# Two recurrent-attention layers with a written-out order: a masked product for the probabilities, half evictions, and another order

## The chip, the cores and the metric

The kernel runs on one core of one Trainium2 chip. The metric is device time in microseconds (us) of one execution; before, three executions took 1612.61, 1614.55 and 1621.16 us. All working below is against the median, 1614.55 us, and against one further execution that was profiled.

## What is computed

Two blocks, A and B, alternate twice (A, B, A, B), each on a layer-normalised input and each with a residual. x has 2048 tokens of 512 channels.

```python
for s in range(n_seg):                       # 64 segments of 32 tokens
    h = concat([mem, x[s]])                  # 8 memory tokens + 32 tokens
    q, k, v = h @ Wq, h @ Wk, h @ Wv         # 32 heads of 128
    p = softmax(where(mask, q @ k.T * scale, -1e9))
    o = (p @ v) @ Wo
    mem = o[:8]                              # feeds the next segment
    out[s] = o[8:]
```

Block B is linear attention: phi(q), phi(k) (where t > 0: t + 1, else exp t), kv = phi(k)^T v, z = sum of phi(k), o = phi(q) kv / (phi(q) z), and an output projection.

Block A is a recurrence: the 8 memory rows that segment s gives are part of the input of segment s + 1. So one segment's projections, its scores for the memory rows, their product with v, the output projection and the transposition of the memory form a chain that is walked 64 times in each layer.

## The kernel before, in words

All four weight matrices of A lie in SBUF. The program is a list of nodes, made by `P.add` with an engine, reads, writes and the PSUM tiles. The table `PLACE` gives each node a number, and, where a node may run on ScalarE (ACT) or VectorE (DVE), a letter, a or v, after it. `schedule` sorts all nodes by that number: it sets the order of each engine's queue, and nothing else; what a node waits for follows from reads, writes and tiles, through semaphores. Every engine runs its queue in order, so a node that waits holds up all that stands behind it on its engine. The file also has costs and latencies beside the nodes (`c_act`, `c_dve`, `lat=`). The program does not read them; they are what the table was made with.

A *step* is one segment. In `PLACE` a key is (layer, step, part). The parts that matter, with the line numbers of the profile:

- **kq0, kq1, v**: `project` (TensorE, L2121 for a weight load with its matmul, L2010 for a matmul with the weights that are there) makes k and q for half of the heads, and v for all. `turned` evicts a PSUM tile (`copy`, L1893 on ACT, L1894 on DVE, 128x512) into one of the buffers `img` and transposes it on DVE (L2139) into kT or qT.
- **mem0, mem1** (`mem_attention`): scores (L2218, L2210), two exponentials on ACT (L2225, L2229), a product with a block mask on DVE (L2233) into Pm, sums over it and the product with v on TensorE (through `tiled`, L2022), a reciprocal by two ACT instructions (L2244, L2246), the memory rows into oTb (DVE, L2258).
- **out**: `out_proj` (L2346): 64 matmuls; TensorE's result has two halves of 64 partitions. One is copied to `outW` (L1893 or L1894), the other added to it by DVE (L2355) into `y_sb`.
- **next**: TensorE (L2372) transposes the memory rows of `y_sb`, and an eviction of 32 columns puts them into the next segment's input.
- **x** (`x_attention`): the tokens' attention, which has until the next step's `out`. DVE masks (L2276), TensorE sums (L2287, L2010), ACT takes the reciprocal (L2290, L2292), DVE multiplies (L2294, L2295). Then the probabilities are put into a block-diagonal buffer `Pbx`: four copies, each of 32 partitions x 256 columns, on ACT or DVE, into a buffer whose other blocks were set to zero once. All product matmuls with v wait for all four copies.
- **res**: the step's rows of y go through DMAs (issued in pairs, by GpSimd, POOL, L1909, and by SyncE, SP) to `dx_sb`; every fourth step the left-over rows are projected too, and DVE adds dx to x (L2416).
- **bi** (`b_in`), once for four steps: `layernorm` of 128 tokens (L2058 to L2064, the last one on DVE), a DMA transpose issued by SP (`turn`, L2049) into xlnT, and four groups of TensorE matmuls, `rows` (L2513, L2010), that read it.
- **prep, left0, left1, leftv** (`prepare`, `left_block`): the same layernorm and transpose for the next four segments, copies of it into their input, and the projections of the last 8 tokens of each segment.
- **bo** (`b_out`): block B's output for the second layer's input.

Of the kernel before, what the change touches and what calls it, by code (L numbers as in the profile page):

```python
# [1548 lines left out]
def c_dve(n, rate=1):  # L1549
    return 0.155 + 1.044e-3 * n / rate  # L1550
# [222 lines left out]
def _build_kernel(nc, A_x, A_mem0, A_Wq, A_Wk, A_Wv, A_Wo, A_seg_len, B_wqkv, B_wo, out):  # L1773
# [274 lines left out]
    def turn(o, i, reads, writes, kind, lat=2.8):  # L2048
        add("sp", lambda e: e.dma_start_transpose(o, i), 1.2, reads=reads, writes=writes, dsem=kind, lat=lat)  # L2049
# [673 lines left out]
```

## Time and profile before

| what | value |
|---|---|
| median of three executions | 1614.55 us (1612.61 to 1621.16) |
| the profiled execution, its own time | 1630.0 us |
| its span, first to last instruction | 1627.4 us |
| granted TensorE clock, mean | 0.998 |
| TensorE (PE) busy | 1534.2 us, 94% |
| DVE busy | 1226.8 us, 75% |
| ACT busy | 1059.4 us, 65% |
| POOL busy | 191.6 us, 12% |

The profiled execution is 15 us longer than the median, of which 2.6 us lie outside its span. Matmuls are pipelined and a busy PE may still hold short waits, so PE's 94% is a share of time with a matmul under way. The waits of PE that are longer than a pipeline gap are named, by what ended them, in the view of waits.

### The profile page before, as it was taken

How to read it: one execution, taken by the hardware profiler on the slowest of the kernel's cores; microseconds unless marked ns; L12 is line 12 of the kernel's file. 1: busy time of each engine (PE TensorE's matmuls, PEld its weight loads, DVE VectorE, ACT ScalarE, POOL GpSimd, SP SyncE). 2: the span in 40 equal slices, each digit the busy share in tenths (PEclk: the TensorE clock that was granted, in tenths of full speed). 3: DMA queues.
4: the chain of work that ended last, by engine and by line, in shares of the span. 5: the costliest groups of instructions: out<-in, count | busy, mean ns of one | idle time of the engine just before them, and what ended most of it. 6: DMA issues, size and time to landing. Idle time of an engine off the chain costs nothing.

```text
span 1627.4 us, 97760 instructions
## 1 busy us (share of the span) xinstructions
PE 1534.2 (94%) x48853; PEld 810.1 (50%) x40499; DVE 1226.8 (75%) x3601; ACT 1059.4 (65%) x3099; POOL 191.6 (12%) x388
## 2 busy tenths in 40 slices
PE   5889999999999999999899999999999999999997
PEld 1445555455555555555444555455555445555453
DVE  3778778877777877777678777777777777777777
ACT  2566666666666667666466677766677667676665
POOL 2011110111111011111101110111110111110110
PEclk9999999999999999999999999999999999999999
DMA  9310000110000001001101101111001110100115
GB/s 382 88 32 23 20 13 22 19 27 20 23 20 14 22 23 23 20 16 24 22 14 19 26 14 25 27 26 23 21 19 23 26 25 19 27 17 21 27 33 145
DMA packets 79348, 58.14 MB, mean 36 GB/s; under 512 B 58872, under 2 KB 73624, under 8 KB 77400
## 3 DMA queue, kind: packets, MB, share of 16 engines
q1 hardware_dynamic: 65912, 36.30, 8.5%
q0 software_dynamic: 12864, 15.46, 3.4%
q8 instruction: 350, 5.73, 1.5%
q14 instruction: 62, 0.51, 0.1%
q10 hardware_dynamic: 160, 0.14, 0.0%
HBM read 25.57 MB, written 10.35 MB: 22 GB/s over the span
## 4 chain that ended last, share of the span: by engine, by line
PE 68%; DVE 13%; DMA 10%; ACT 7%; issue 2%; POOL 0%; SPq 0%; DVEq 0%
PE pb L2121 25%; PE pb L2010 17%; PE pb L2346 12%; PE pb L2022 8%; DMA arena_sb<-arena_sb 5%; DVE arena_sb L1894 3%; ACT arena_sb L1893 2%; DMA dx_sb<-y_sb 2%; DMA Wv_sb<-in_A_Wv_dram 2%; DVE arena_sb L2139 2%; PE pb L2513 2%; PE pb L2210 1%; DVE y_sb L2355 1%; DVE arena_sb L2294 1%; PE pb L2372 1%
## 5 line engine op out<-in xcount | busy, mean ns | idle before, releaser
L1893 ACT ACTIVATE arena_sb<-pb 128x512 bf16<-128x512 f32 (+4 forms) x1032 | 499.6, 511 | 293.1 <-PE pb L2010 131.5
L1894 DVE CAST arena_sb<-pb 128x512 bf16<-128x512 f32 (+3 forms) x614 | 322.3, 533 | 105.7 <-PE pb L2010 64.9
L2121 PE MATMUL pb<-Wk_sb,arena_sb 128*32 128x512 bf16 x4096 | 363.3, 381 | 8.2 <-DMA Wk_sb<-in_A_Wk_dram 4.3
L2346 PE MATMUL pb<-Wo_sb,arena_sb 128*32 128x256 bf16 x10368 | 340.0, 273 | 5.7 <-issue 3.3
L2139 DVE STREAM_TRANSPOSE arena_sb<-arena_sb 128x256 f32<-128x256 f32 x640 | 263.3, 431 | 55.0 <-ACT arena_sb L1893 49.0
L2346 PEld LDWEIGHTS pb<-Wo_sb,arena_sb 128*32 128x32 bf16 x10368 | 257.7, 96 | 53.5 <-issue 15.9
L2022 PE MATMUL pb<-arena_sb 128*32 128x128 bf16 (+2 forms) x10800 | 266.6, 209 | 18.3 <-DVE arena_sb L1894 10.0
L2121 PE MATMUL pb<-Wq_sb,arena_sb 128*32 128x512 bf16 x3072 | 266.9, 379 | 3.3 <-DVE arena_sb L1894 2.8
L1909 POOL DMA_DIRECT2D dx_sb<-y_sb x252 | 128.4, 513 | 1198.5 <-DVE y_sb L2355 776.5
L2022 PEld LDWEIGHTS pb<-arena_sb 128*32 128x32 bf16 x10800 | 183.5, 96 | 149.5 <-DVE arena_sb L1894 45.5
L2121 PE MATMUL pb<-Wv_sb,arena_sb 128*32 128x512 bf16 x2560 | 251.4, 378 | 2.3 <-ACT arena_sb L1893 1.2
L2010 PE MATMUL pb<-Wv_sb,arena_sb 128*32 128x512 bf16 x2560 | 251.2, 378 | 0.0
L2121 PEld LDWEIGHTS pb<-Wk_sb,arena_sb 128*32 128x32 bf16 x4096 | 110.5, 97 | 196.4 <-issue 97.3
L2010 PE MATMUL pb<-Wq_sb,arena_sb 128*32 128x512 bf16 x2048 | 200.7, 379 | 0.0
L1893 ACT ACTIVATE arena_sb<-arena_sb 32x256 bf16<-32x256 bf16 (+2 forms) x411 | 146.9, 361 | 38.8 <-DVE arena_sb L2294 29.1
L2121 PEld LDWEIGHTS pb<-Wq_sb,arena_sb 128*32 128x32 bf16 x3072 | 83.8, 96 | 93.6 <-issue 43.6
L1894 DVE COPY arena_sb<-arena_sb 32x256 bf16<-32x256 bf16 (+2 forms) x502 | 100.8, 203 | 20.6 <-DMA arena_sb<-arena_sb 11.3
L2355 DVE TENSOR_TENSOR y_sb<-pb,outW_sb 64x256 bf16<-64x256 f32 x162 | 67.8, 419 | 55.4 <-ACT outW_sb L1893 51.3
L2258 DVE TENSOR_TENSOR arena_sb<-pb,arena_sb 128x128 bf16<-128x128 f32 x252 | 73.1, 290 | 47.3 <-PE pb L2022 15.2
L2121 PEld LDWEIGHTS pb<-Wv_sb,arena_sb 128*32 128x32 bf16 x2560 | 70.1, 95 | 66.1 <-issue 36.9
L2010 PE MATMUL pb<-Wk_sb,arena_sb 128*32 128x512 bf16 x1024 | 101.6, 379 | 0.0
L1893 ACT ACTIVATE outW_sb<-pb 64x256 f32<-64x256 f32 x130 | 49.0, 377 | 73.5 <-PE pb L2346 71.3
(110 smaller groups left out, 1793.2 us busy)
## 6 DMA issues: line engine op xcount, KB each, us to landing
Wk_sb<-in_A_Wk_dram SPq DMA_DIRECT2D x1, 4096.0 KB, 13.7
Wq_sb<-in_A_Wq_dram SPq DMA_DIRECT2D x1, 4096.0 KB, 24.1
Wv_sb<-in_A_Wv_dram SPq DMA_DIRECT2D x1, 4096.0 KB, 33.5
Wo_sb<-in_A_Wo_dram SPq DMA_DIRECT2D x16, 256.0 KB, 7.3
xs_scratch<-x_sb POOLq DMA_DIRECT2D x32, 128.0 KB, 2.2
pq_scratch<-arena_sb POOLq DMA_DIRECT2D x31, 128.0 KB, 2.4
x_sb<-xs_scratch POOLq DMA_DIRECT2D x16, 128.0 KB, 3.0
dx_sb<-y_sb SPq DMA_DIRECT2D x126, 12.0 KB
```

Of the source, the lines that this page charges most:

```text
L1893: return e.activation(o() if callable(o) else o, i() if callable(i) else i, ACTF.Copy)
L1894: return e.tensor_copy(o() if callable(o) else o, i() if callable(i) else i)
L1909: add(eng, lambda e: e.dma_start(o, i), 0.55 if eng == "pool" else 0.66, reads=reads, writes=writes, dsem="%s%d" % (kind, k), lat=lat + (0 ...
L2010: return pe.add_instruction(mybir.InstMatmult(name=nc.get_next_instruction_name(), engine=mybir.EngineType.PE, ins=[pe.lower_ap(x), pe.low ...
L2022: r = pe.matmul(o[q], w[:, q], x, start=start, stop=stop, skip_group_check=True, tile_position=(0, 32 * j))
L2121: r = pe.matmul(o, blk[:, c, :], w, start=(c == 0), stop=(c == 3), tile_position=(0, 32 * j))
L2139: add("dve", lambda v: v.transpose(dst, src(img[:, k, :].bitcast(F32))), 0.445, reads=[("img", k)], writes=[dkey])
L2210: r = pe.matmul(o, kT[:, hh, j // 2, :, j % 2], qT[:, hh, j // 2, :, j % 2].rearrange("p (k x) -> p k x", k=5), start=True, stop=True, til ...
L2258: add("dve", lambda v: v.tensor_tensor(oTb[:, s % NO, 16 * b:16 * b + 16, 0:8].rearrange("p (i j) q -> p j i q", i=4), heads(pv.f32()[:, 0 ...
L2346: r = pe.matmul(tl.f32()[32 * j:32 * j + 32, 0:256], oT[:, 4 * hh + n, :], Wo_sb[:, 8 * n + hh, 256 * d:256 * d + 256], start=(hh == 0 and ...
L2355: add("dve", lambda e: e.tensor_tensor(y_sb[0:64, k, :], tl.f32()[a, 0:256], outW[c, v, :], ALU.add), c_dve(256), reads=[("outW", w)], til ...
L2513: r = pe.matmul(dst.f32()[q, :], xlnT[:, c, q], wqkv_sb[:, c, o:o + D], start=c == 0, stop=c == 3, skip_group_check=True, tile_position=(0 ...
```

## The change

1. **Masked product.** In `x_attention` the four copies into `Pbx` are replaced by two DVE products, one for each half of the heads: px, repeated over four blocks, times the block mask `bo_sb`, repeated over four groups of columns; 128 partitions x 512 columns each. The zeros are now written each time, so the zeroing of `Pbx` at the start goes. A half's product matmuls wait for that half's product alone.
2. **Output halves.** In `out_proj` the half that is copied to `outW` and the half that DVE adds change places (also for the left-over rows).
3. **Half evictions.** The second q projection of a step (kq1) is evicted in two instructions of 256 columns; each has its own letter. All buffers `img` get a key for each half.
4. **Order.** 1506 of the 1509 lines of `PLACE` are new, and with them many of the engines' letters. The latencies beside the transposes were 2.8 and are 3.6, and 4.4 for that of `b_in`.
5. The transposes of `b_out` wait on four semaphores in turn in place of one.

```diff
-    (0, 1, 'kq1'): '51206 51638 51854 52285 51422 52070 52501 52717 52709a 53955 53856a 54093',
+    (0, 1, 'kq1'): '51422 52774 52775 52776 49480 51638 51854 52070 53425a 53782 52773a 52493a 54145',
...
-    def turn(o, i, reads, writes, kind, lat=2.8):
-        add("sp", lambda e: e.dma_start_transpose(o, i), 1.2, reads=reads, writes=writes, dsem=kind, lat=lat)
+    def turn(o, i, reads, writes, kind, lat=3.6):
+        add("sp", lambda e: e.dma_start_transpose(o, i), 1.2, reads=reads, writes=writes, dsem=kind, lat=4.4 if kind == "dtb" else lat)
...
-        def turned(tl, dst, dkey, urgent, src=None):
+        def turned(tl, dst, dkey, urgent, src=None, parts=1):
             k = slot_img(urgent)
-            nd = evac(img[:, k, :].rearrange("p (n f e) -> p n f e", f=32, e=2),
-                      lambda: tl.f32()[:, :].rearrange("p (n e f) -> p n f e", f=32, e=2), 512, tiles=[tl],
-                      writes=[("img", k)])
+            for h in range(parts):
+                n = 512 // parts
+                nd = evac(img[:, k, n * h:n * h + n].rearrange("p (n f e) -> p n f e", f=32, e=2),
+                          lambda h=h, n=n: tl.f32()[:, n * h:n * h + n].rearrange("p (n e f) -> p n f e", f=32, e=2), n, tiles=[tl],
+                          writes=[("img", k, h)] if parts > 1 else [("img", k, 0), ("img", k, 1)])
             src = src or (lambda v: v)
             add("dve", lambda v: v.transpose(dst, src(img[:, k, :].bitcast(F32))), 0.445,
-                reads=[("img", k)], writes=[dkey])
+                reads=[("img", k, h) for h in range(2)], writes=[dkey])
...
-            for j in range(4):
-                q = slice(32 * j, 32 * j + 32)
-                add(ANY, copy(Pbx[q, j, :, :], px[q]),
-                    {"act": c_act(256, 0, 1), "dve": c_dve(256, 4)}, quad=(j, j), reads=pk + [("Px", r2)], writes=[("Pbx", j)])
+            for b in range(2):
+                add("dve", lambda v, b=b: v.tensor_tensor(
+                    Pbx[:, :, b, :].rearrange("p j (k x) -> p j k x", k=4),
+                    px[:, b, :].rearrange("p (k x) -> p k x", k=4).unsqueeze(1).to_broadcast([128, 4, 4, 32]),
+                    bo_sb[:, :].rearrange("p (j x) -> p j x", j=4).unsqueeze(2).to_broadcast([128, 4, 4, 32]), ALU.mult),
+                    c_dve(512, 2), reads=pk + [("Px", r2), "bo"], writes=[("Pbx", b)])
...
-                        reads=[("Pbx", j) for j in range(4)] + [("v", r2, b)] + ([("vl", g2, b), "Pbl"] if i == 3 else []),
+                        reads=[("Pbx", b), ("v", r2, b)] + ([("vl", g2, b), "Pbl"] if i == 3 else []),
...
-            a, c = (slice(0, 64), slice(64, 128))[::1 if urgent else -1]
+            a, c = (slice(0, 64), slice(64, 128))[::-1 if urgent else 1]
...
-            add("dve", lambda v: v.memset(Pbx[:, :, :, :].rearrange("p j b x -> p (j b x)").bitcast(F32), 0.0), 0.7,
-                writes=[("Pbx", j) for j in range(4)])
...
-                turned(tq, pairs(qT[:, 4 * b:4 * b + 4])[:, :, 0:32], ("qT", b), True)
+                turned(tq, pairs(qT[:, 4 * b:4 * b + 4])[:, :, 0:32], ("qT", b), True, parts=1 + b)
...
-            turn(e, pq_view[t], [("pq", t)], ek, "dtq")
+            turn(e, pq_view[t], [("pq", t)], ek, "dtq%d" % (t % 4))
```

The letters as the two tables have them, for both layers: the copies into `Pbx` stood 228 times on ACT and 284 times on DVE, and the 256 products all stand on DVE. Evictions of 128x512 stood 657 times on ACT and 303 times on DVE and now stand 554 and 278 times there; of the 256 half evictions 224 stand on ACT and 32 on DVE. In 99 of the 128 steps both halves stand on ACT, in 26 one on each engine, in 3 both on DVE.

More of the change, by code (lines that the diff above doesn't have):

```diff
@@ L2156, in left_block @@
                 k = slot_img(False)
-                evac(img[:, k, :], lambda tl=tl: tl.f32()[:, :], 512, tiles=[tl], writes=[("img", k)])
+                evac(img[:, k, :], lambda tl=tl: tl.f32()[:, :], 512, tiles=[tl], writes=[("img", k, 0), ("img", k, 1)])
                 add("dve", lambda v, k=k: v.transpose(
@@ L2160, in left_block @@
                     img[:, k, :].bitcast(F32).rearrange("p (i d f) -> p d i f", i=4, d=2)), 0.445,
-                    reads=[("img", k)], writes=["vtmp"])
+                    reads=[("img", k, 0), ("img", k, 1)], writes=["vtmp"])
                 add("dve", lambda v, b=b: v.transpose(vleft[:, r2, b].rearrange("p g d -> p (g d)").bitcast(F32), vtmp.bitcast(F32)),
@@ L2351, in out_proj @@
             k = int(w == NW - 1)
-            a, c = (slice(0, 64), slice(64, 128))[::1 if urgent else -1]
+            a, c = (slice(0, 64), slice(64, 128))[::-1 if urgent else 1]
             v = w if urgent else 0
-            evac(outW[c, v, :], lambda: tl.f32()[c, 0:256], 256, tiles=[tl], writes=[("outW", w)])
+            nd = evac(outW[c, v, :], lambda: tl.f32()[c, 0:256], 256, tiles=[tl], writes=[("outW", w)])
+            nd.quad = (0, 0) if urgent else (2, 2)
             add("dve", lambda e: e.tensor_tensor(y_sb[0:64, k, :], tl.f32()[a, 0:256], outW[c, v, :], ALU.add),
-                c_dve(256), reads=[("outW", w)], tiles=[tl], writes=[("y", k)])
+                c_dve(256), reads=[("outW", w)], tiles=[tl], writes=[("y", k)], quad=(2, 0) if urgent else (2, 1))
             return k
```

3010 rows, old and new, of the table PLACE are left out of this document.

## The prediction

> **What bounds the kernel now.** I read the page first, then busy time by stretch, then what PE waited for. On the page, the chain that ended last is mostly PE, and PE has work nearly all the time.
>
> ```profile
> PE 1534.2 (94%) x48853; PEld 810.1 (50%) x40499; DVE 1226.8 (75%) x3601; ACT 1059.4 (65%) x3099; POOL 191.6 (12%) x388
> ...
> PE 68%; DVE 13%; DMA 10%; ACT 7%; issue 2%; POOL 0%; SPq 0%; DVEq 0%
> ```
>
> The change leaves PE's work as it is: no matmul is added or taken away. So only PE's idle time can be won, or more of it made. Busy time by stretch tells where it lies; PE's is the first number after the length.
>
> ```profile
> 0.00:20.00 20.00, 6.87 (x105) 1.88 (x67) 6.28 (x16) 3.65 (x12) 10.90 (x42) 1.00 0.91 369
> 20.00:40.00 20.00, 16.58 (x348) 3.93 (x168) 6.80 (x21) 6.25 (x19) 0.00 (x0) 1.00 1.03 396
> 40.00:60.00 20.00, 16.36 (x508) 8.83 (x416) 15.21 (x44) 9.16 (x27) 0.00 (x0) 1.00 0.63 185
> ...
> 1560.00:1600.00 40.00, 34.27 (x1100) 18.25 (x920) 27.42 (x78) 18.93 (x53) 4.70 (x9) 1.00 0.42 84
> 1600.00:1627.40 27.40, 21.22 (x528) 11.12 (x528) 24.43 (x43) 18.98 (x33) 0.00 (x0) 0.90 0.40 128
> sum 1627.40, PE 1534.20 PEld 810.11 DVE 1226.78 ACT 1059.43 POOL 191.63; mean PE 73.06 PEld 38.58 DVE 58.42 ACT 50.45 POOL 9.13
> ```
>
> PE is idle 1627.4 - 1534.2 = 93.2 us. Of these 60 - 39.8 = 20.2 lie in the first 60 us, where the weights land (DMA share near 1), and 67.4 - 55.5 = 11.9 in the last 67. The change hardly touches either. **61 us in the 1500 us between** are what it works on. What ended those waits:
>
> ```profile
> PE pb L2513 <- DMA arena_sb<-arena_sb: 14.4, 13, 1.9
> PE pb L2022 <- DVE arena_sb L1894: 10.0, 28, 1.3
> ...
> PE pb L2372 <- DVE y_sb L2355: 6.1, 20, 0.8
> ...
> PE pb L2218 <- DVE arena_sb L2139: 4.2, 8, 1.3
> PE pb L2121 <- DVE arena_sb L1894: 4.0, 7, 1.3
> PE pb L2022 <- ACT arena_sb L1893: 3.9, 12, 0.6
> ...
> PE pb L2022 <- DVE arena_sb L2233: 1.9, 7, 0.4
> ...
> PE pb L2121 <- ACT arena_sb L1893: 1.7, 3, 1.2
> ```
>
> The largest is no engine: `rows` (L2513) waits for the DMA transpose of the normalised tokens. PE's timeline shows one case: the out block's 64 matmuls, then nothing until the transpose has landed, and `next` (L2372) behind it in the queue.
>
> ```profile
> 1027.06 1.93 PE L2346 MATMUL pb<-Wo_sb,arena_sb 128*32 128x256 bf16 x64
> 1029.97 0.40 PE L2513 MATMUL pb<-arena_sb 128*32 128x512 bf16 x4 [0.98 <-DMA arena_sb<-arena_sb]
> ...
> 1031.92 0.21 PE L2372 MATMUL pb<-selm_sb,y_sb 128*32 128x16 bf16 x8
> ```
>
> **The change part by part.** I count from the two tables how much PE work stands in the queue between a cause and its reader (the *cover*), each instruction at its own rate in the chain: 32 matmuls of a projection 1.73 us, 64 of an out block 1.75.
>
> ```profile
> 118.16 1.75 PE pb L2346 x64
> 123.63 1.73 PE pb L2121 x32
> ```
>
> *Transpose of `b_in`.* From the last DVE instruction of the layernorm to the first `rows`, the 28 transposes inside the steps had a cover of 1.73 to 3.22 us, mean 2.63; now 3.02 to 4.87, mean 3.65. The transposes take
>
> ```profile
> 103.17 5.03 DMA arena_sb<-arena_sb
> ...
> 770.88 4.50 DMA arena_sb<-arena_sb
> ...
> 1220.30 3.30 DMA arena_sb<-arena_sb
> ```
>
> 3.3 us when quick and 4.5 to 5.0 when slow. One more us of cover takes about 1 of each of the 13 waits, which are 1.1 on average and 1.9 at most: 14.4 falls to about 3.4. I take -11; bounds 0 (the wait turns up elsewhere, see the rivals) and -14.4.
>
> *Transpose of `prepare`.* Cover to the first copy of it: mean 3.99 before, 4.99 after.
>
> ```profile
> DVE arena_sb L1894 <- DMA arena_sb<-arena_sb: 11.3, 8, 3.0
> ```
>
> Here DVE stands, and PE's projections behind its copies: at most the 4.0 + 1.7 us that L2121 waits for evictions and copies. I take -3, bounds 0 and -5.7.
>
> *Masked product.* Its rows:
>
> ```profile
> L1893 ACT ACTIVATE arena_sb<-arena_sb 32x256 bf16<-32x256 bf16 x228 | 94.3, 414 | 33.3 <-DVE arena_sb L2294 29.1
> L2233 DVE TENSOR_TENSOR arena_sb<-arena_sb 128x256 bf16<-128x256 bf16 x252 | 70.2, 279 | 16.1 <-ACT arena_sb L2225 13.6
> L1894 DVE COPY arena_sb<-arena_sb 32x256 bf16<-32x256 bf16 x284 | 62.2, 219 | 8.2
> L2416 DVE TENSOR_TENSOR x_sb<-x_sb,dx_sb 128x512 bf16<-128x512 bf16 x30 | 12.1, 405 | 7.1 <-DMA dx_sb<-y_sb 5.2 <-issue 1.8
> L2655 DVE TENSOR_TENSOR arena_sb<-arena_sb 128x512 bf16<-128x512 bf16 x16 | 10.8, 676 | 0.1
> ```
>
> A 128x512 bf16 product with repeated operands isn't in the trace. Half its size with the same kind of repetition (L2233) takes 279 ns; its size in bf16 alone (L2416) 405; its size with an f32 operand (L2655) 676. I take 405. DVE: +256 x 0.405 - 62.2 = +41.5 us; ACT: -94.3. With the other moves of evictions at the durations 685 and 596 (25 fewer on DVE, 103 fewer on ACT) and the halves below, DVE ends near +25, ACT near -57 us.
>
> ```profile
> L1893 ACT ACTIVATE arena_sb<-pb 128x512 bf16<-128x512 f32 x678 | 391.6, 596 | 222.3 <-PE pb L2010 131.5 <-PE pb L2121 26.1 <-PE pb L2022 22.3
> L1894 DVE CAST arena_sb<-pb 128x512 bf16<-128x512 f32 x326 | 222.6, 685 | 81.5 <-PE pb L2010 64.9 <-PE pb L2121 6.2 <-PE pb L2218 4.7
> ```
>
> For PE only delay counts. In one step of before,
>
> ```profile
> 711.04 0.43 DVE L2294 TENSOR_TENSOR arena_sb<-arena_sb 128x256 bf16<-128x256 bf16 x1
> ...
> 712.08 1.29 ACT L1893 ACTIVATE arena_sb<-arena_sb 32x256 bf16<-32x256 bf16 x3
> ...
> 713.42 0.24 PE L2022 MATMUL pb<-arena_sb 128*32 128x128 bf16 x4 [0.20 <-ACT arena_sb L1893]
> ```
>
> the last copy ended 1.9 us after px (711.47 to 713.37). Two products end 0.81 after px, and a half's matmuls may start after 0.41. The tables spend this: cover from the sums to those matmuls falls from 4.33 to 3.81 us (first half, mean) and 5.05 to 4.70 (second). So I take -2 of the 13.9 us that L2022 waits for L1894 and L1893 (copies and evictions of v together); bounds -13.9, and +7, by which covers under 2.6 us fall short more than before (13.5 against 6.6 us, summed).
>
> [...]
>
> *Half evictions.*
>
> ```profile
> L2290 ACT ACTIVATE arena_sb<-pb 128x256 f32<-128x256 f32 x128 | 48.2, 377 | 13.7 <-PE pb L2010 12.7
> ```
>
> Two halves on ACT take 2 x 377 = 754 ns in place of 596: 0.16 later in 99 steps; on two engines about 0.2 earlier in 26. The cover from this projection to the scores rises by 0.12 (2.18 to 2.30). I take 0; bounds -4.2 and +4.2, what L2218 waits now. [...]
>
> *Other places of the order.* Scores to sums: cover in mem0 1.60 to 1.45; `out` to `next` 1.06 to 1.03; v to its reader, those under 0.8 us fall short by 11.7 against 9.4, summed. `out` to `next`, under 1.0: 12.2 against 9.0. I take +5; bounds 0 and +12.
>
> *At nothing:* the output halves (same shapes, one row each), the semaphores of `b_out`, the zeroing that goes (in the first 20 us, DVE busy 6.28). If that cover goes, each costs under 1 us. SP and POOL issue as many DMAs as before.
>
> **Sum**: -11 - 3 - 2 + 0 + 5 = -11 us; on the profiled execution 1630.0 becomes 1619, on the median 1614.55 becomes **1603.5**. Bounds: -38 and +23.
>
> **Rivals.**
>
> *The wait moves (no change).* In the timeline `next` stands behind `rows`: while PE waits for the transpose, `y` gets ready. Put other work there, and PE may wait for y (6.1 us now) or the next input instead. For: the chain of a segment has to be walked anyway. Against: `rows` and the other work are both free to fill that time. If the 14 us of DMA terms come back, -2 + 5 = +3: 1617.5.
>
> *DVE holds up the chain (slower).* A pair of products holds DVE 0.81 us a step, against 284 / 128 x 0.219 = 0.49. If a transpose (L2139), a memory row or `y` stands behind it in DVE's queue, PE's next projection is up to 0.32 us late: over 126 steps +41. It outweighs the 14 us of DMA gain from one step in three; at two in three, +27 - 14 + 3 - 2 = +14: 1628. For: DVE is 75% busy and ended PE's waits for L1894, L2355, L2139 and L2233 above. Against: ACT is relieved by twice as much, and what the products lead to isn't read before the next step's out block (cover from the first half's last matmul to it 4.66 us before and 4.92 after, mean).
>
> [...]
>
> **How the numbers follow.** About 0.5% (8 us) is what a measurement of this kernel can tell from no change. Forecast 0.50, the wait moves 0.25, DVE holds up the chain 0.21, slow product 0.04. The forecast's own range is 1591 to 1606; the range for 8 in 10 reaches to the rivals at 1617.5 and 1628 and leaves out the slow product and the bounds' far ends, which need every cover to go one way: 1591 to 1628. Faster 0.50, same 0.25, slower 0.25.
>
> **What would show it.** L2513's wait for the DMA under 5 us; product rows near 405 ns; halves near 377; DVE near 1252 us and ACT near 1002 busy; PE busy unchanged at 1534; PE idle near 82. Wrong would be: waits of L2372, L2218 or L2022 that grow by what L2513 loses (first rival), or DVE as the releaser of clearly more than the 26 us that the rows of PE's waits above put on it (second).

## The result, and the profile after

| what | before | after |
|---|---|---|
| median of four executions | 1614.93 us (1612.61 to 1621.16) | 1599.14 us (1597.58 to 1601.09) |
| ratio of the times, 95% interval | | 0.9897 (0.9867 to 0.9927) |
| the profiled execution, its own time | 1630.0 us | 1597.58 us |
| its span | 1627.4 us | 1595.8 us |

The kernel became 15.8 us faster (1.0%); the forecast was 11. Most lines of the program have moved by a few: `rows` is now L2516, `next` L2377, the DVE add into y L2360, the scores L2220 and L2212, the transposes L2141, the mask product into Pm L2235, the new product L2300, the residual add L2421. First the page after, engines and chain:

```profile
PE 1527.5 (96%) x48853; PEld 816.7 (51%) x40499; DVE 1227.3 (77%) x3543; ACT 975.2 (61%) x3028; POOL 191.6 (12%) x388
...
PE 78%; DVE 9%; DMA 5%; ACT 4%; SPq 2%; issue 1%; POOL 1%; DVEq 0%; ACTq 0%
```

The same 48853 matmul instructions are there. PE is idle 1595.8 - 1527.5 = 68.3 us in place of 93.2, and the chain that ended last runs through PE for 78% of the span in place of 68%: DMA's share halves (10% to 5%), DVE and ACT lose 4 and 3 points. Busy time by stretch (the first number after the length is PE's) says where:

```profile
0.00:20.00 20.00, 6.89 (x97) 1.64 (x59) 5.16 (x16) 3.48 (x12) 10.94 (x42) 1.00 0.91 370
20.00:40.00 20.00, 16.26 (x340) 3.81 (x168) 7.97 (x21) 4.96 (x15) 0.00 (x0) 1.00 1.04 395
40.00:60.00 20.00, 18.10 (x561) 9.24 (x449) 15.27 (x44) 10.25 (x31) 0.00 (x0) 1.00 0.57 184
60.00:1530.00 1470.00, 1431.60 (x46248) 772.46 (x38376) 1147.67 (x3346) 920.41 (x2889) 174.80 (x335) 1.00 0.09 22
```

In the stretch from 60 us to the last 66 the idle time is 1470.0 - 1431.6 = 38.4 us, against 61.1 in the 1500 us of before; so 22.7 of the 24.9 us come from the steady stretch. What PE waited for after (us in total, times, longest):

```profile
PE pb L2377 <- DVE y_sb L2360: 7.2, 18, 0.8
...
PE pb L2220 <- DVE arena_sb L2141: 3.8, 5, 2.4
PE pb L2022 <- DVE arena_sb L2235: 3.0, 10, 0.6
...
PE pb L2022 <- DVE arena_sb L1894: 2.5, 9, 0.5
...
PE pb L2022 <- ACT arena_sb L1893: 1.4, 4, 0.7
...
PE pb L2121 <- ACT arena_sb L1893: 1.4, 2, 1.2
...
PE pb L2022 <- DVE arena_sb L2300: 1.3, 5, 0.4
...
PE pb L2121 <- DVE arena_sb L1894: 0.7, 2, 0.4
```

The row that led this view before, `rows` waiting for a DMA (14.4 us in 13 waits), is gone: no row has L2516 behind a DMA. L2022 waits 2.5 + 1.4 us for evictions, and 1.3 for the products that replaced the copies, together 5.2 in place of 13.9. The 13.9 of before are two things under the same two lines: by the shape of the instruction that ended each wait, the copies into `Pbx` (32x256) make 4.0 + 1.6 = 5.6 us of it and the evictions of v (128x512) 6.0 + 2.2 = 8.2. So 4.3 us fell away with the copies, and the other 4.3 are a shorter wait for v. `next` waits 7.2 for y in place of 6.1.

The prediction's execution of before was 15 us above its median, so a second one of each kernel serves for the accounts below: 1623.88 us for before (the median of the executions beside it was 1622.17) and 1602.41 for after (median beside it 1605.61). The same view of them, before first:

```profile
PE pb L2022 <- DVE arena_sb L1894: 9.6, 27, 1.3
PE pb L2513 <- DMA arena_sb<-arena_sb: 9.0, 10, 1.5
...
PE pb L2372 <- DVE y_sb L2355: 5.7, 18, 0.8
PE pb L2022 <- ACT arena_sb L1893: 4.5, 14, 0.6
...
PE pb L2346 <- issue: 3.7, 8, 1.1
PE pb L2121 <- DVE arena_sb L1894: 3.4, 7, 0.9
```

And after:

```profile
PE pb L2377 <- DVE y_sb L2360: 7.4, 18, 0.8
...
PE pb L2350 <- issue: 5.2, 10, 1.3
...
PE pb L2022 <- DVE arena_sb L1894: 2.5, 8, 0.5
PE pb L2121 <- ACT arena_sb L1893: 2.3, 3, 1.2
```

In an execution near the median of before the wait for the transposes is 9.0 us, not 14.4. Adding up all rows of this view by the waiting line, down to 0.2 us, gives an account of the second pair:

| waiting line on PE | before | after | change |
|---|---|---|---|
| `rows` (L2513, L2516) | 11.6 | 1.5 | -10.1 |
| products and sums through `tiled` (L2022) | 26.3 | 17.9 | -8.4 |
| weight loads of projections (L2121) | 11.0 | 6.9 | -4.1 |
| `next` (L2372, L2377) | 5.7 | 7.6 | +1.9 |
| out blocks (L2346, L2350) | 5.0 | 7.3 | +2.3 |
| scores (two lines) | 4.3 | 5.6 | +1.3 |
| all lines | 76.3 | 60.5 | -15.8 |

Three of these rows hold more than one thing. In `tiled`, the copies' 5.6 us became 1.3 for the products, and the evictions of v went from 8.5 to 3.9. In L2121, 2.7 of the 4.1 us are the wait for the weights to land in the first 60 us (5.9 to 3.2). The out blocks' +2.3 is mostly `issue`, gaps for which the profile names no cause (3.7 to 5.2); in the first pair the out blocks show 4.6 and 4.5, so this one is within what two executions of a kernel differ by.

The span fell by 1622.1 - 1600.7 = 21.4 us: 15.6 of PE's idle time and 5.8 of its busy time (1534.6 to 1528.8).

### The profile page after: what moved, and what is told of

The parts are those of the page before. It is cut to its first block, busy times and chain, and to the rows that moved or that the text cites. A ratio compares the mean times of both kernels' runs of the same rounds, so it can differ in the third digit from the quotient of the medians.

```text
span 1595.8 us, 97632 instructions
## 1 busy us (share of the span) xinstructions
PE 1527.5 (96%) x48853; PEld 816.7 (51%) x40499; DVE 1227.3 (77%) x3543; ACT 975.2 (61%) x3028; POOL 191.6 (12%) x388
## 4 chain that ended last, share of the span: by engine, by line
PE 78%; DVE 9%; DMA 5%; ACT 4%; SPq 2%; issue 1%; POOL 1%; DVEq 0%; ACTq 0%
PE pb L2121 28%; PE pb L2010 20%; PE pb L2350 17%; PE pb L2022 8%; DMA dx_sb<-y_sb 3%; SPq L1924 2%; PE pb L2516 2%; ACT arena_sb L1893 1%; DVE arena_sb L1894 1%; PE pb L2212 1%; DVE arena_sb L2141 1%; DVE y_sb L2360 1%; PE pb L2289 1%; ACT outW_sb L1893 1%; DMA arena_sb<-arena_sb 1%
## 5 line engine op out<-in xcount | busy, mean ns | idle before, releaser
L1893 ACT ACTIVATE arena_sb<-pb 128x512 bf16<-128x512 f32 (+5 forms) x1173 | 520.2, 478 | 353.9 <-PE pb L2010 186.5
L1894 DVE CAST arena_sb<-pb 128x512 bf16<-128x512 f32 (+4 forms) x597 | 307.9, 524 | 103.6 <-PE pb L2010 64.0
L2121 PE MATMUL pb<-Wk_sb,arena_sb 128*32 128x512 bf16 x4096 | 362.1, 380 | 4.7 <-DMA Wk_sb<-in_A_Wk_dram 2.3
L2350 PE MATMUL pb<-Wo_sb,arena_sb 128*32 128x256 bf16 x10368 | 338.8, 273 | 5.5 <-issue 2.3
L2141 DVE STREAM_TRANSPOSE arena_sb<-arena_sb 128x256 f32<-128x256 f32 x640 | 264.0, 431 | 45.9 <-ACT arena_sb L1893 39.3
L2350 PEld LDWEIGHTS pb<-Wo_sb,arena_sb 128*32 128x32 bf16 x10368 | 258.7, 96 | 54.2 <-DVE arena_sb L2260 14.9
L2022 PE MATMUL pb<-arena_sb 128*32 128x128 bf16 (+2 forms) x10800 | 275.5, 208 | 9.2 <-DVE arena_sb L1894 2.5
L2121 PE MATMUL pb<-Wq_sb,arena_sb 128*32 128x512 bf16 x3072 | 265.6, 379 | 1.3 <-DVE arena_sb L1894 0.7
L2022 PEld LDWEIGHTS pb<-arena_sb 128*32 128x32 bf16 x10800 | 187.2, 95 | 139.2 <-issue 29.3
L2121 PE MATMUL pb<-Wv_sb,arena_sb 128*32 128x512 bf16 x2560 | 251.5, 378 | 1.7 <-ACT arena_sb L1893 1.2
L2121 PEld LDWEIGHTS pb<-Wk_sb,arena_sb 128*32 128x32 bf16 x4096 | 110.2, 96 | 188.6 <-issue 92.6
L2121 PEld LDWEIGHTS pb<-Wq_sb,arena_sb 128*32 128x32 bf16 x3072 | 83.8, 96 | 97.0 <-issue 47.0
L1893 ACT ACTIVATE outW_sb<-pb 64x256 f32<-64x256 f32 x138 | 52.2, 378 | 102.3 <-PE pb L2350 85.2
L2360 DVE TENSOR_TENSOR y_sb<-pb,outW_sb 64x256 bf16<-64x256 f32 x162 | 68.7, 424 | 47.3 <-ACT outW_sb L1893 41.8
L2300 DVE TENSOR_TENSOR arena_sb<-arena_sb,bo_sb 128x512 bf16<-128x512 bf16 x256 | 101.9, 416 | 2.4
L2121 PEld LDWEIGHTS pb<-Wv_sb,arena_sb 128*32 128x32 bf16 x2560 | 70.5, 96 | 57.8 <-issue 29.3
L2235 DVE TENSOR_TENSOR arena_sb<-arena_sb 128x256 bf16<-128x256 bf16 x252 | 69.9, 280 | 19.3 <-ACT arena_sb L2227 17.0
```

The costliest lines, as they stand in the source:

```text
L1893: return e.activation(o() if callable(o) else o, i() if callable(i) else i, ACTF.Copy)
L1894: return e.tensor_copy(o() if callable(o) else o, i() if callable(i) else i)
L2022: r = pe.matmul(o[q], w[:, q], x, start=start, stop=stop, skip_group_check=True, tile_position=(0, 32 * j))
L2121: r = pe.matmul(o, blk[:, c, :], w, start=(c == 0), stop=(c == 3), tile_position=(0, 32 * j))
L2141: add("dve", lambda v: v.transpose(dst, src(img[:, k, :].bitcast(F32))), 0.445, reads=[("img", k, h) for h in range(2)], writes=[dkey])
L2235: add("dve", lambda v: v.tensor_tensor(Pm[:, k, :].rearrange("p (a j x) -> p a j x", a=2, j=4), PQ[:, r2, b, 0:64].rearrange("p (a x) -> p ...
```

## The experiments

The theory was that the new order lets the transposes land before `rows` needs them, and that the product matters little; the rivals were that the product, or the relief of ACT, brings the gain. Each kernel's ratio is against the kernel before, run beside it; intervals are 95%.

**The new order with the old code.** Four copies stand at the places of the two products, the first of each pair on DVE and the second on ACT, the second pair moved ahead of its first reader where it must be; q evictions are whole.

```diff
...
+        elif k[2] == "x":
+            t, u = sorted(e[0] for e in v[6:8])
+            u = min(u, v[9][0] - 1, v[14 + (k[1] < 63)][0] - 1)
+            v[6:8] = [(t, "dve"), (t, "act"), (u, "dve"), (u, "act")]
...
```

> The new order with the old code: four copies into Pbx (two on DVE and two on ACT, at the two products' places, moved ahead of the first matmul that reads them), whole evictions, output halves as before. If the gain comes from the order (longer cover of the transposes), most of it is here: 0.991 to 0.996 of before, and PE waits for the DMA in front of the rows under 4 us. If it comes from the masked product and the relief of ACT, this one is 0.998 or above, and the waits of L2022 for copies and evictions stay near 13.9 us.

1661.82 us against 1623.92: 1.0233 (1.0211 to 1.0255). What PE waited for, and the copies on ACT (lines 14 higher; L1907 is an ACT copy, L2036 a matmul of `tiled`):

```profile
PE pb L2036 <- ACT arena_sb L1907: 28.8, 38, 3.0
PE pb L2386 <- DVE y_sb L2369: 9.5, 21, 0.9
PE pb L2036 <- DVE y_sb L2369: 9.0, 12, 1.4
```

```profile
L1907 ACT ACTIVATE arena_sb<-arena_sb 32x256 bf16<-32x256 bf16 x256 | 106.0, 414 | 43.5 <-DVE arena_sb L2308 38.2
```

The order alone is no gain: it is a loss of 2.3%. The first expectation is missed, and of the second only the time holds, for the waits of `tiled` for copies and evictions grew to 28.8 + 5.2 us (the second row is L1908, copies and evictions on DVE). `rows` waits for no DMA here either, so the order by itself takes that wait away; yet matmuls wait 28.8 us for ACT, up to 3.0 us at a time, 26.2 of it for copies. My reading is that this order was made for a product that is ready earlier.

**The new code in the old order.** The products stand at the places of the first and third copy; both q halves on the whole eviction's engine.

```diff
...
+        if k[2] == "kq1":
+            v.insert(11, v[10])
+        elif k[2] == "x":
+            t = sorted(e[0] for e in v[6:10])
+            v[6:10] = [(t[0], None), (t[2], None)]
...
```

> The old order with the new code: two products at the first and the third of the four copies' places, both halves of the eviction on the engine of the whole one, output halves changed. If the gain is the order's, 0.997 to 1.004 of before, with the rows' wait for the DMA still at 8 to 15 us. If it is the product's, 0.990 to 0.995, with the waits of L2022 for L1894, L1893 and the product under 7 us.

1624.4 us against 1623.92: 0.9999 (0.9985 to 1.0013). PE's waits (lines 13 to 18 higher; L2363 is an out block, L2390 `next`, L2529 `rows`, L2313 the product):

```profile
PE pb L2363 <- issue: 9.5, 20, 1.1
PE pb L2390 <- DVE y_sb L2373: 8.9, 28, 0.8
...
PE pb L2529 <- DMA arena_sb<-arena_sb: 5.7, 8, 1.3
PE pb L2035 <- DVE arena_sb L1907: 5.2, 14, 0.9
...
PE pb L2035 <- ACT arena_sb L1906: 2.6, 8, 0.8
...
PE pb L2035 <- DVE arena_sb L2313: 2.2, 6, 0.6
```

The code does shorten what it touches: `tiled` waits 20.2 us in all its rows, not 26.3, and ACT is busy 960.6 us, some 99 less. There are no copies here, so the rows split the 13.9 us: 2.2 for the products in place of 5.6 for copies, and 5.2 + 2.6 = 7.8 for evictions of v, as before. But `next` waits 3.2 us more for y and the out blocks 6.6 more; all rows together are 79.0 us against 76.3. So the win is lost elsewhere, with `next` in the chain of the segment; 9.5 us of the out blocks' 11.6 are `issue`, and what they wait for stays open. In the old order the products and the relief of ACT are worth nothing, and neither part alone is the change: together they give -1.1%, one by one +2.3% and 0. The time is in the first expectation's range, but the rows' wait for the DMA is 5.7 us and not 8 to 15: at the same cover of 2.63 us it was 14.4, 9.0 and 5.7 us in three executions.

**More cover alone.** In the kernel before, the residual add and the layernorm of `b_in`, with their DMAs, stand up to 1 us sooner in the queues (mean cover 3.46 us in place of 2.63).

```diff
...
+    _v[0:5] = [(max(t - _n, _r[20][0] + 1 + _i), e) for _i, (t, e) in enumerate(_v[0:5])]
+    _v[5] = (max(_v[4][0] + 1, _v[5][0] - _n), None)
```

> The kernel before with one thing moved: the residual add and the layernorm of b_in stand up to 1 us sooner in the queues (the row DMAs ahead of them too), so the cover of the transpose is 3.46 us in the mean in place of 2.63. If that cover is what the rows' wait hangs on, the wait falls under 5 us and the time to 0.993 to 0.997 of before. If the wait only moves to another place (y or the next input), the time is within 0.2% of before while the wait at the rows is gone.

1661.13 us against 1623.92: 1.0228 (1.0204 to 1.0252). The rows' wait falls under 5 us, as the first expectation had it, but the time misses both. PE's waits, then DVE's (L2228 are the scores, L2426 the residual add; the profiled execution is the shortest of five, 1654.32 us):

```profile
PE pb L2228 <- DVE arena_sb L2149: 18.5, 27, 2.1
PE pb L2382 <- DVE y_sb L2365: 13.2, 23, 2.8
```

```profile
DVE x_sb L2426 <- DMA dx_sb<-y_sb: 27.8, 20, 3.1
```

`rows` waits only 1.5 us for the DMA, but DVE now stands 27.8 us before the residual add (5.2 before), because y's rows haven't come back through the DMAs. The transposes (L2149) and y, which the chain needs, are DVE's work too, and PE's waits for them are what grew: 18.5 us in place of 4.2 or 2.4, and 13.2 in place of 6.1 or 5.7. Here the cover bought by moving a waiting instruction forward was paid on its engine.

**Less cover in the kernel after.** Only the layernorm of `b_in` stands 1 us later (mean cover 2.87 us in place of 3.65).

```diff
...
+    _v[0:6] = [(min(t + _n, _v[7][0] - 6 + _i), e) for _i, (t, e) in enumerate(_v[0:6])]
```

> The changed kernel with one thing moved back: the layernorm of b_in stands 1 us later in the queues, cover 2.87 us in the mean in place of 3.65. If the cover is the cause, the rows wait for the DMA again by 5 to 13 us, and the time is 0.993 to 0.998 of before in place of 0.990. If the gain is elsewhere, it stays at 0.989 to 0.991.

1629.97 us against 1623.92: 1.0037 (1.0022 to 1.0053), 1.4% above the kernel after; the wait is in the expected range, the time is not. PE's waits (L2521 is `rows`, L2240 makes Pm, L2217 are scores; the profiled execution is the shortest of twelve, 1624.58 us):

```profile
PE pb L2521 <- DMA arena_sb<-arena_sb: 9.5, 8, 2.6
PE pb L2027 <- DVE arena_sb L2240: 8.0, 20, 1.1
...
PE pb L2217 <- DVE arena_sb L2146: 5.9, 11, 1.0
```

The wait for the transposes comes back at 9.5 us, as it should where cover decides. The loss is over twice that: all rows together are 82.2 us in place of 60.5, `tiled` alone 26.5 in place of 17.9. PE's waits for Pm (8.0 us in place of 2.9) and for the transposes before the scores (10.2 in place of 5.6) grew, both DVE's work; my reading is that the layernorm, now later, stands in front of them.

**The kernel after again, beside the next three.**

> The changed kernel once more, unchanged, as the measure for the three beside it, each of which undoes one part of the new code and keeps the new order. 0.987 to 0.993 of before; no wait of the rows for the DMA.

1605.61 us against 1622.71: 0.9893 (0.9875 to 0.9912), the first result again.

**DVE copies in place of the products.** In the kernel after, each product becomes two DVE copies, all matmuls wait for all four, and the second pair is moved ahead of the first reader.

```diff
...
-                add("dve", lambda v, b=b: v.tensor_tensor(
...
+                for j in range(2 * b, 2 * b + 2):
+                    q = slice(32 * j, 32 * j + 32)
+                    add("dve", copy(Pbx[q, j, :, :], px[q]), c_dve(256, 4), reads=pk + [("Px", r2)], writes=[("Pbx", j)])
...
```

> The changed kernel with four copies into Pbx again, all on DVE, two at each product's place: 4 x 0.22 = 0.88 us of DVE where the two products take 0.83. If the order and the place of this work on DVE make the time, it is within 0.3% of after_again. If the product as such does, by a half's matmuls that wait for that half alone, it is slower by 0.5% or more and the waits of L2022 for DVE grow by over 5 us. The run with the new order and two of the copies on ACT took 1.0233 of before; if ACT's late copies were the cause there, this one doesn't show it.

1632.44 us: 1.0057 (1.0042 to 1.0073), 1.6% above the kernel after. PE's wait (L1901 is a copy on DVE), and the copies' row:

```profile
PE pb L2029 <- DVE arena_sb L1901: 24.8, 57, 1.5
```

```profile
L1901 DVE COPY arena_sb<-arena_sb 32x256 bf16<-32x256 bf16 x512 | 111.8, 218 | 14.3
```

Four copies cost DVE about what two products do (4 x 218 = 872 ns against 2 x 416 = 832), and no ACT is in the way. `tiled` waits 41.2 us in all rows, 23.3 more, 22.2 of it for copies. The order with two of its copies on ACT took 1.0233, so ACT's late copies were about half of the 3.4% between that run and the kernel after.

**Products that must both be ready.** Both products stay, but each half's matmuls wait for both; in 53 of the 128 steps the second one has to be moved ahead for that.

```diff
...
-                        reads=[("Pbx", b), ("v", r2, b)] + ([("vl", g2, b), "Pbl"] if i == 3 else []),
+                        reads=[("Pbx", 0), ("Pbx", 1), ("v", r2, b)] + ([("vl", g2, b), "Pbl"] if i == 3 else []),
```

> The changed kernel with both products, but every product matmul with v waits for both, as it waited for all four copies; where the second product stood behind the first such matmul in the order, it is put just ahead of it. If what the masked product brings is that a half's matmuls wait for that half alone, this is 1.003 to 1.007 of before, like the run with four copies on DVE (1.0057), with 15 to 25 us of waits of L2022 for the product. If the copies as such were the loss there (32 partitions at a time, 0.05 us more a step), this stays at 0.988 to 0.992.

1613.2 us against 1622.17: 0.9934 (0.9915 to 0.9954), 0.4% above the kernel after; the two intervals don't overlap. This lies between the two expectations, nearer to the second. PE's waits (L2305 is the product):

```profile
PE pb L2027 <- DVE arena_sb L2305: 10.7, 26, 1.3
```

`tiled` waits 10.7 us for products in place of 1.3, and 27.9 in place of 17.9 in all rows. So about a quarter of the 1.6% is that a half waits for its own product alone. The rest lies with the copies and the places to which they had to be moved; these two weren't told apart.

**Whole q evictions.**

```diff
+    if _k[2] == "kq1":
+        del _v[11]
...
-                turned(tq, pairs(qT[:, 4 * b:4 * b + 4])[:, :, 0:32], ("qT", b), True, parts=1 + b)
+                turned(tq, pairs(qT[:, 4 * b:4 * b + 4])[:, :, 0:32], ("qT", b), True)
```

> The changed kernel with the second q projection evicted whole, on the engine of the first half, at its place: 0.60 us on ACT in place of 2 x 0.38. If the halves only fit what is there, 0.2% faster to 0.2% slower than after_again. If they matter by letting the transpose start sooner where they stand on two engines (26 of 128 steps), slower by 0.2 to 0.5%.

1603.79 us: 0.9881 (0.9865 to 0.9897). No difference from 0.9893 can be told.

**Output halves back.**

```diff
-            a, c = (slice(0, 64), slice(64, 128))[::-1 if urgent else 1]
+            a, c = (slice(0, 64), slice(64, 128))[::1 if urgent else -1]
```

> The changed kernel with the output halves as before: the other 64 partitions are copied and added. The instructions keep their shapes, so within 0.2% of after_again. A rival: which half an engine reads sets the length of the copy or of the sum, then the row of y differs from 424 ns by over 20 ns and the time by over 0.3%.

1608.29 us: 0.9904 (0.9888 to 0.992). No difference can be told, and the row of y is 419 ns against 424.

**The wait taken away from either kernel.** `rows` reads a constant tile in place of xlnT, so it waits for no transpose; the kernel leaves out block B's input.

```diff
...
-                add("pe", mm, c_pe(len(parts), 512), reads=["wqkv", "xlnT"], tiles=[p[1] for p in parts])
+                add("pe", mm, c_pe(len(parts), 512), reads=["wqkv", "xlnT" if end else "one"], tiles=[p[1] for p in parts])
```

> The kernel before, but the rows of b_in read a constant tile in place of the transposed tokens (but for the last tokens of each layer), so they never wait for the DMA, which is still issued; the kernel leaves out block B's input. What the wait costs is then the whole difference: 0.991 to 0.994 of before (10 to 14 us) by the profile that I predicted from; 0.996 to 1.000 if PE's wait there is time in which it would wait for y or the next input anyway.

1609.87 us against 1622.17: 0.9925 (0.9907 to 0.9942), or 12.3 us less. PE's waits there:

```profile
PE pb L2022 <- DVE arena_sb L1894: 10.5, 30, 1.3
...
PE pb L2372 <- DVE y_sb L2355: 5.5, 17, 0.8
```

The others are about as before: all rows together are 63.0 us in place of 76.3, and no line waits longer than in the longer of the two executions of before. The wait was worth its whole length, and by the medians a little more (12.3 us against 9.0).

> The same substitution in the changed kernel (block B's input left out). Its profile shows no wait of the rows for the DMA, so 0.988 to 0.991 of before, no other than the changed kernel itself. If it is faster than that by 0.3% or more, the transposes still cost something that the waits don't show.

1600.67 us: 0.9863 (0.9846 to 0.988), just below the expected range and 0.3% below the kernel after, which ran beside other executions of before; the intervals just overlap. If the transposes still cost something after the change, it is about that.

**The kernel before, profiled once more.**

> The kernel before, unchanged, for a second profile: the first one was of an execution 15 us above the median. The rows' wait for the DMA is between 5 us (as in the run with the old order and the new code) and 14.4 us; under 8 us means that the first profile showed more of it than a usual execution has.

1623.88 us; the rows wait 9.0 us for the DMA, between the two bounds. Its waits stand in the section on the result.

## Why the prediction was right, and where it wasn't

**Transpose of b_in (-11): right.** Waits of `rows` fell by 10.1 us in the second pair and the DMA's row is gone, in the order alone too; taking the wait from the kernel before is worth 12.3 us, and giving 0.8 us of cover back brings 9.5 us of it back. The direction is shown. That one us of cover is worth one us of each wait is not: the eight waits that came back at 2.87 us of cover are up to 2.6 us long, longer than any at 2.63 before. The prediction took 3.3 us for a quick transpose, from three rows of the chain. In the view of DMAs of before the median from issue to landing is 2.8 us (for these transposes and those of `prepare`), and PE's view of waits lists 13 waits for the 30 transposes, so most of them needed no more cover.

```profile
arena_sb<-arena_sb SPq DMA_TRANSPOSE x59, 2.8
```

What the prediction could not see is that 14.4 us were more than the 9.0 of a second execution. That -11 lies so near the measured 10.1 is in part luck.

**Transpose of `prepare` (-3): of the right size.** DVE's own wait for this transpose was 11.3 us in 8 waits before; after, its row is

```profile
DVE arena_sb L1894 <- DMA arena_sb<-arena_sb: 1.1, 3, 0.5
```

PE's L2121 waits for evictions and copies 5.7 us before and 2.1 after in the first profiles (-3.6), 4.5 and 3.1 in the second (-1.4). No run takes this part alone.

**Masked product (-2): this term was mis-sized.** Its duration was right: 405 ns were taken, and the row shows

```profile
L2300 DVE TENSOR_TENSOR arena_sb<-arena_sb,bo_sb 128x512 bf16<-128x512 bf16 x256 | 101.9, 416 | 2.4
```

416 ns. What failed is the step "The tables spend this": I took -2 because the covers became shorter, 4.33 to 3.81 us and 5.05 to 4.70. But the first half's product ends sooner by more than that. DVE's timeline shows a step of after: px, product, a small product for the memory rows, product.

```profile
704.72 0.42 DVE L2296 TENSOR_TENSOR arena_sb<-arena_sb 128x256 bf16<-128x256 bf16 x1 [0.16 <-ACT arena_sb L2294]
705.18 0.42 DVE L2300 TENSOR_TENSOR arena_sb<-arena_sb,bo_sb 128x512 bf16<-128x512 bf16 x1
705.52 0.22 DVE L2297 TENSOR_TENSOR arena_sb<-arena_sb 128x64 bf16<-128x64 bf16 x1
705.66 0.42 DVE L2300 TENSOR_TENSOR arena_sb<-arena_sb,bo_sb 128x512 bf16<-128x512 bf16 x1
```

From px's end at 705.14 the first half is ready after 0.46 us and the second after 0.94, against 1.9 us for four copies in the prediction's example. Over all 128 steps the four copies were ready 2.05 us after px in the mean (median 1.53), the first product 0.72 (0.46) and the second 1.80 (1.07). So the first half won 1.3 us for 0.5 of cover spent, and the second only about what it spent, 0.25 for 0.35. The wait for copies, 5.6 of the 13.9 us, fell by 4.3 to the 1.3 for products, in both pairs: that is the measure of this term, about twice the -2. The experiments agree that it counts: copies back cost 1.6%, waiting for both products 0.4%.

**Half evictions and output halves (0): right**, within what can be told. Two halves on ACT take a little less than the 754 ns I reckoned:

```profile
L1893 ACT ACTIVATE arena_sb<-pb 128x256 bf16<-128x256 f32 x224 | 77.0, 384 | 36.6 <-PE pb L2121 20.5 <-DVE arena_sb L1894 7.4 <-PE pb L2022 4.0
```

224 x 384 ns are 86.0 us, the row counts 77.0: halves that follow each other overlap, by an estimated 9.0 / 99 = 0.09 us a pair if it is all in the 99 steps, so a pair takes near 2 x 0.384 - 0.09 = 0.68 us; the pair at 721.49 in ACT's timeline takes 0.66. That is 0.68 - 0.596 = 0.08 us more than a whole eviction, where the forecast had 0.16.

**Other places of the order (+5): too high, by v.** `next`, the out blocks and the scores wait 1.9 + 2.3 + 1.3 = 5.5 us more in the second pair (3.7 in the first). But the same term held v to its reader, which was to get worse (11.7 us short against 9.4, summed). The wait for evictions of v got better: 8.2 us to 3.9 in the first pair, 8.5 to 3.9 in the second. It goes with the order: it is 3.5 to 5.5 us in every run with the new one, and 7.8 to 8.5 with the old one, but for 5.2 where the layernorm was moved. What in the new order does it no run takes apart. With it the term is near +1 in the second pair, not +5: counting the shortfall of covers did not price this wait.

**The sum.** -10.1 - 4.1 - 8.4 + 5.5 = -17.1 us by the account, and the smaller lines bring it to -15.8; the medians fell by 15.8 and 17.1. The forecast was -11. By its own terms the 5 to 6 us between are the evictions of v (-4.6, forecast as a part of +5), the product (-4.3 in place of -2) and the wait for the weights at the start (-2.7, which the prediction took as hardly touched), less what the transposes fell short of -14 (-10.1 - 1.4). So the mechanism was right for the largest term, and that the errors of the others left the time inside the range is in part luck. I had treated the terms as separate, and this the runs refute: the code alone takes 3.4 us of the copies' wait and wins no time, the order alone takes all of the rows' wait for the DMA and loses 2.3%.

**The rivals.** *The wait moves* did not happen to the change (`next` +1.9 and the scores +1.3 against 10.1 at `rows`), but the code alone in the old order looks like it (`next` +3.2, out blocks +6.6). *DVE holds up the chain* did not happen either: the rows that put 26 us on DVE before add to 2.5 + 7.2 + 3.8 + 0.7 + 3.0 = 17.2 after, and all rows that DVE ended to 38.0 in place of 40.6. It is what the kernel with more cover alone did (+2.3%). Its forecast has a slip: +27 - 14 + 3 - 2 counts the product's -2 twice, since the +3 has it already; it should have been +16, near 1631 and not 1628. The *slow product*, one that takes L2655's 676 ns, did not come: the row shows 416 ns.

**What was to show it.** The row for the DMA is under 5 us, the product near 405 ns, the halves near 377 (384). Three signs didn't come true. PE's busy time is 1527.5, not 1534, and its idle time 68 us, not 82. DVE is busy 1227 us, not 1252, and ACT 975, not 1002. Of these two the work was reckoned rightly: row by row DVE gains 101.9 - 62.2 - 18.6 + 12.9 - 14.3 (smaller rows) = 19.7 (forecast 25) and ACT loses 62 (57). The terms that the prediction shows come to about +37 and -71; the smaller evictions that changed engine, which make them +25 and -57, it doesn't list. The page, though, counts the time of overlapping instructions once: in the timeline above L2297 starts at 705.52 and the product before it ends at 705.60. All rows of DVE add to 1375.0 us after, 148 more than the page's busy time; before, the difference is 129. A forecast of a busy share from a sum of durations was too high here for that reason.

## What to carry to other kernels

Where a queue's order is written out by hand, price a faster operation by when its reader can start, not by its duration: the same products were worth 0 in one order and 1.6% in the other (against copies put at their places), and the order without them cost 2.3%. Split a row of waits by the shape of what ended them before putting a price on it: half of the 13.9 us here was not the copies'. More time between a transfer and its reader was no gain here where it was bought by moving forward an instruction that waits itself: the rows' wait fell from 14.4 or 9.0 us to 1.5, DVE's before the residual add rose from 5.2 to 27.8, and the time grew by 2.3%. So see what would stand behind it on its engine. Before rebuilding an order, let the reader take a constant once, to measure what its wait is worth (12.3 us here).

## What was not expected of the hardware

**DVE waited longer for y's rows in a faster kernel and in a slower one.** After the change DVE waits three to four times as long for the rows of y (21.2 and 17.0 us in the two executions, 5.2 and 5.5 before), and PE's waits shrank all the same:

```profile
DVE x_sb L2421 <- DMA dx_sb<-y_sb: 21.2, 16, 3.7
```

With 27.8 us in the kernel with more cover alone, PE's wait for the transposes went from 4.2 to 18.5 us, and the time up by 2.3%. The size of the wait alone did not tell its cost in these two; that what stands next in the queue decides is my reading, and no run tests it by itself.

**PE's busy time isn't constant for the same matmuls.** It was 1527.5 and 1528.8 us in the two executions after, 1534.2 and 1534.6 in those before, and 1547.4 in the order with the old code (granted clock 0.996 there, 0.998 to 1.000 in the other four). Matmuls overlap in the trace: in PE's timeline of before, four of 0.39 us start at 711.45 and the next four at 711.67. One place where the difference may hide is the weight loads, which wait while PE still counts as busy (the first profiles, before, then after):

```profile
PEld pb L2022 <- DVE arena_sb L1894: 45.9, 94, 2.0
...
PEld pb L2022 <- ACT arena_sb L1893: 18.2, 47, 1.3
```

```profile
PEld pb L2022 <- DVE arena_sb L1894: 20.4, 59, 0.7
...
PEld pb L2022 <- DVE arena_sb L2300: 16.6, 53, 0.6
...
PEld pb L2022 <- ACT arena_sb L1893: 10.3, 32, 1.2
```

64.1 us for evictions and copies became 47.3 for evictions and products, where the matmuls of L2022 wait 13.9 and 5.2 us for the same. That the 6 to 7 us of busy time come from there was not tested.
